# A fused long-convolution and SwiGLU kernel under another hand-written order of its operations

## The chip, the cores and the metric

The kernel runs on one core of a Trainium2 chip. The metric is the device time of one execution in microseconds (us); lower is better. The engines are TensorE (PE in the profile, its weight loads PEld), VectorE (DVE), ScalarE (ACT), GpSimd (POOL) and SyncE (SP); the last two issue the transfers here. Each engine works through its own instructions in order, and waits on semaphores for the others.

## The reference

All data are bf16; there are S = 2048 rows of D = 640 channels, and the hidden width of the second part is F = 1728.

```python
# A: shift convolution, long convolution, gate
k_shift = sum of 4 taps: k[t - i] * shift_k[:, i]
kv = k_shift * v
y  = irfft(rfft(kv, 2S) * rfft(ssm_k, 2S))[:S]   # causal convolution of 2048 taps, per channel
y  = y + kv * ssm_D
h  = q + layernorm(q) * y
# B: feed-forward
x2 = layernorm(h)
out = h + (silu(x2 @ w_gate) * (x2 @ w_up)) @ w_down
```

## The kernel before, in words

The sequence is cut into four blocks of 512 rows (`BLK`), block j = 0 to 3. Instead of one long FFT, each block of `ssm_k` and of `kv` has a spectrum of its own, made by matrix products with a cosine and sine matrix `WF`, and output block j sums the products of the spectra X_i and H_(j-i). In the names, G_j is the spectrum of block j of `ssm_k`, X_j that of block j of `kv`, and H_j is G_j joined with G_(j-1) (`window`, L463 and L467).

Per block the work is:

- `g_turned` brings a block of `ssm_k` with time on the partitions: for block 0 by TensorE transposes (L411) and evictions (L413), for the others by a ScalarE copy (L419, one instruction of 2560 columns) and transposing transfers.
- `kv_of` makes the shift convolution on TensorE (`taps`, L490) and multiplies by `v` on VectorE (L513 in block 0; else ScalarE eviction L511 and product L515).
- `transform` makes a spectrum: TensorE products (`forward`, L329) into a PSUM tile, and an eviction (`taken`, L319 on ScalarE, L322 if VectorE does it). Block 0 is done in two halves of 320 columns, `w0` and `w1`; the "first X eviction" is that of X0's tile c = 2 in half `w0`. Sums of halves are L361, L379, L386, L390 and L393 on VectorE.
- `mac` multiplies spectra on VectorE (L537 to L594; most products are 128x2560, L542 and L545).
- `inverse` goes back (TensorE L698), ScalarE scales by the first layer norm (L707), VectorE multiplies by q less its mean and so forms h (L709), ScalarE sums squares (L606), and VectorE and GpSimd make the second norm's statistics (L644, L646, L610, L648).
- `turn_h` normalises a row tile of h (L722 on ScalarE, or L724 if VectorE does it) and turns it into hT, by TensorE transposes with ScalarE evictions (L413) in blocks 0 and 3, by transposing transfers in blocks 1 and 2.
- `ffn` makes gate and up products (TensorE L769), SiLU (ScalarE L783), moves `up` out of PSUM (ScalarE L785) and multiplies on VectorE (L787); as an alternative VectorE multiplies straight from PSUM (L786) and L785 falls away. Then comes the down product (L833, L845), and the rows leave with an accumulating transfer (L850, L852), or at the end over L862, L864 and L866. The feed-forward part of block j lies among the convolution of block j+1.

Before all that stand some small preparations: `fold` (L886, L887) makes a small identity from the large one for the diagonal tap matrices (`tapw` L896, `diag` L897), and `negated` (L912) makes copies of `WF` and `WI` with the sign changed.

Nothing of this is emitted where it is written. `Plan.add` records 923 operations, and `Plan.run` emits them along the hand-written table `ORDER`; the order of the instructions on every engine is that of the table. A negative entry i is operation ~i run in its alternative form (another engine, or for L785 the product straight from PSUM). Buffers are given out along the same table, the one longest free first: four PSUM tiles of two banks (`ps`), five row tiles, three `sg` tiles and 22 units of a large SBUF array (`arena`). So the order of the table also sets which operation waits for which buffer.

## Time and profile before

| | |
|---|---|
| time, three runs | 252.25, 251.06 and 252.71 us; median 252.25 |
| profiled execution | 251.19 us, of which the span from first to last instruction is 249.5 us |
| TensorE busy | 237.7 us, 95% of the span |
| VectorE busy | 197.6 us, 79% |
| ScalarE busy | 174.0 us, 70% |
| GpSimd busy | 52.4 us, 21% |
| granted TensorE clock | 1.00 |
| read from and written to HBM | 16.29 MB and 4.59 MB |

A row of the timeline gives start, duration, engine, line, operation, tiles and shapes, and in brackets the idle time of the engine just before with what ended it. Neighbouring instructions of one line may share a row (x2 and so on). Matrix products overlap in the pipeline, so that the row of several ends a little after the next row begins. Idle time of an engine that nobody waits for costs nothing.

### The profile page before, as it was taken

How to read it: one execution, taken by the hardware profiler on the slowest of the kernel's cores; microseconds unless marked ns; L12 is line 12 of the kernel's file. 1: busy time of each engine (PE TensorE's matmuls, PEld its weight loads, DVE VectorE, ACT ScalarE, POOL GpSimd, SP SyncE). 2: the span in 40 equal slices, each digit the busy share in tenths (PEclk: the TensorE clock that was granted, in tenths of full speed). 3: DMA queues.
4: the chain of work that ended last, by engine and by line, in shares of the span. 5: the costliest groups of instructions: out<-in, count | busy, mean ns of one | idle time of the engine just before them, and what ended most of it. 6: DMA issues, size and time to landing. Idle time of an engine off the chain costs nothing.

```text
span 249.5 us, 5148 instructions
## 1 busy us (share of the span) xinstructions
PE 237.7 (95%) x2125; PEld 152.5 (61%) x2125; DVE 197.6 (79%) x250; ACT 174.0 (70%) x300; POOL 52.4 (21%) x53
## 2 busy tenths in 40 slices
PE   3899988999999999999999999999999999999994
PEld 3467655888857766544466676454456785464662
DVE  2779998999999999999999899999999542131222
ACT  2399998999999977969598699984532865325100
POOL 0002002531230313124400503353702110000030
PEclk9999999999999999999999999999999999999999
DMA  6999899287998566690725569789592200000052
GB/s 204 353 264 144 229 342 355 65 208 114 143 297 283 167 99 130 109 206 6 119 43 133 105 94 216 132 155 162 97 206 29 26 0 3 0 0 3 0 79 79
DMA packets 37283, 33.66 MB, mean 135 GB/s; under 512 B 22470, under 2 KB 32076, under 8 KB 37260
## 3 DMA queue, kind: packets, MB, share of 16 engines
q1 hardware_dynamic: 32028, 22.03, 34.0%
q0 software_dynamic: 5232, 11.31, 25.4%
q8 instruction: 16, 0.26, 0.4%
q14 instruction: 7, 0.06, 0.1%
HBM read 16.29 MB, written 4.59 MB: 84 GB/s over the span
## 4 chain that ended last, share of the span: by engine, by line
PE 75%; ACT 9%; DMA 6%; DVE 6%; issue 2%; SPq 1%; DVEq 0%; ACTq 0%
PE ps L769 36%; PE ps L845 23%; PE ps L329 7%; PE ps L698 5%; ACT arena L319 4%; DMA arena<-in_A_ssm_k_dram 4%; DMA arena<-arena 3%; PE ps L490 2%; DVE arena L542 2%; PE ps L833 1%; PE ps L411 1%; ACT arena L419 1%; DVE tT L787 1%; ACT sg L783 1%; ACT row L722 1%
## 5 line engine op out<-in xcount | busy, mean ns | idle before, releaser
L769 PE MATMUL ps<-arena,wgu 128*128 128x512 bf16 (+1 forms) x680 | 118.2, 329 | 0.4 <-ACT arena L413 0.2
L769 PEld LDWEIGHTS <-wgu 128*128 128x128 bf16 x680 | 66.2, 98 | 45.0 <-issue 1.1
L845 PE MATMUL ps<-wd,tT 128*128 128x320 bf16 x416 | 59.1, 299 | 0.0
L845 PEld LDWEIGHTS <-tT 128*128 128x128 bf16 x416 | 39.8, 98 | 17.2 <-issue 1.6
L542 DVE TENSOR_TENSOR arena<-arena 128x2560 bf16<-128x2560 bf16 x30 | 43.9, 1486 | 0.2
L783 ACT ACTIVATE sg<-ps 128x1024 bf16<-128x1024 f32 (+1 forms) x28 | 27.1, 971 | 22.2 <-PE ps L769 22.0
L329 PE MATMUL ps<-arena,WF 128*128 128x320 bf16 x176 | 29.8, 299 | 1.7 <-ACT arena L319 0.9
L785 ACT CAST sg<-ps 128x1024 bf16<-128x1024 f32 (+1 forms) x24 | 23.6, 982 | 8.5 <-PE ps L769 3.6
L610 POOL TENSOR_TENSOR sm<-sm,neghalf 128x4 f32<-128x4 f32 (+1 forms) x10 | 17.9, 1793 | 42.9 <-DVE sm L646 42.6
L243 POOL DMA_DIRECT2D arena<-arena x11 | 13.4, 1218 | 60.7 <-DVE arena L542 27.6
L319 ACT CAST arena<-ps 128x640 bf16<-128x640 f32 (+1 forms) x47 | 24.8, 594 | 1.3 <-PE ps L329 1.0
L787 DVE TENSOR_TENSOR tT<-sg,sg 128x1024 bf16<-128x1024 bf16 (+1 forms) x24 | 15.9, 664 | 11.0 <-ACT sg L785 11.0
L329 PEld LDWEIGHTS <-WF 128*128 128x128 bf16 x176 | 17.1, 97 | 11.1 <-issue 2.7
L545 DVE TENSOR_TENSOR arena<-arena 128x2560 bf16<-128x2560 bf16 x14 | 20.8, 1488 | 0.2
L606 ACT ACTIVATE junk<-arena 128x640 bf16<-128x640 bf16 x28 | 20.6, 745 | 0.4 <-DVE arena L709 0.4
L319 ACT ACTIVATE arena<-ps 128x640 bf16<-128x640 f32 (+1 forms) x32 | 19.8, 654 | 0.8 <-PE ps L329 0.8
L698 PE MATMUL ps<-arena,WI 128*128 128x320 bf16 x96 | 15.8, 299 | 1.0 <-issue 0.8
L709 DVE SCALAR_TENSOR_TENSOR arena<-arena,sm,ps 128x640 bf16<-128x640 bf16 x16 | 13.7, 877 | 3.2 <-ACT ps L707 3.1
L850 ACT ACTIVATE row<-ps,sm 128x640 bf16<-128x640 f32 x12 | 9.5, 791 | 8.6 <-PE ps L845 8.1
L852 POOL DMA_DIRECT2D out_dram<-row x12 | 11.7, 1151 | 14.6 <-ACT row L850 14.6
L707 ACT ACTIVATE ps<-ps,sm 128x640 f32<-128x640 f32 x16 | 11.9, 767 | 3.4 <-PE ps L698 3.3
L698 PEld LDWEIGHTS <-WI 128*128 128x128 bf16 x96 | 9.0, 97 | 5.6 <-issue 1.8
(91 smaller groups left out, 236.8 us busy)
## 6 DMA issues: line engine op xcount, KB each, us to landing
arena<-arena POOLq DMA_DIRECT2D x11, 640.0 KB, 6.2
arena<-in_A_v_dram SPq DMA_DIRECT2D x4, 640.0 KB, 5.1
arena<-in_A_q_dram SPq DMA_DIRECT2D x4, 640.0 KB, 4.5
out_dram<-row POOLq DMA_DIRECT2D x13, 160.0 KB, 4.2
arena<-in_A_ssm_k_dram SPq DMA_DIRECT2D x3, 640.0 KB, 8.8
wd<-in_B_w_down_dram SPq DMA_DIRECT2D x2, 800.0 KB, 7.1
out_dram<-arena POOLq DMA_DIRECT2D x2, 640.0 KB, 5.9
wgu<-in_B_w_gate_dram SPq DMA_DIRECT2D x1, 800.0 KB, 5.9
```

The lines of the kernel that those rows point to most:

```text
L319: (lambda: nc.scalar.activation(dst(), src(), ACT.Copy, scale=2.0)) if twice else (lambda: nc.scalar.copy(dst(), src())),
L329: nc.tensor.matmul(ap(ps)[:, h, 0:NH], w, ap(src)[:, r, h * NH:(h + 1) * NH], start=(first and i == 0), stop=(last and i == len(rs) - 1), ...
L542: dve(1402, lambda: v.tensor_mul(to(), X.part(xs), H.part(hs)), [X.at(xs), H.at(hs)], [at])
L545: added(1402 * n - 69 * (n - 1), lambda: v.tensor_add(to(), to(), b()), to, b, [what], at, n)
L606: act(725, lambda r=r: nc.scalar.activation(waste(), ap(x)[:, r, :], ACT.Square, scale=D ** -0.5, accum_out=sm(s, MSQ, (r,))), [(x, r)], [ ...
L610: nc.gpsimd.tensor_tensor(sm(s, RSTD, rs), sm(s, VAR, rs), ap(neghalf)[:, 0:len(rs)], op=ALU.pow)
L698: nc.tensor.matmul(ap(ps)[:, w, 0:NH], m, src[:, w * NH:(w + 1) * NH], start=(i == 0), stop=(i == len(terms) - 1))
L769: nc.tensor.matmul(split(ap(ps), n)[:, i, :], w(k), ap(hT)[:, k, lo:lo + n], start=(k == 0), stop=(k == KT - 1))
L783: act(905 if wide_ else 490, lambda: nc.scalar.activation(of(sg), of(*gate), ACT.Silu), [(gate[0], gate[1] + i) for i in range(m)] + (psu ...
L785: op = plan.add("act", 905 if wide_ else 490, lambda: nc.scalar.copy(of(co), of(*up)), psu + [sg], [co] + tt, ("dve", 1135 if wide_ else 6 ...
L787: op.rest = dve(602 if wide_ else 336, lambda: nc.vector.tensor_mul(to(), of(sg), of(co)), [sg, co], tt)
L845: nc.tensor.matmul(ap(ps[hf])[:, hf, 0:NH], ap(tT)[:, c * BLK + at:c * BLK + at + P], ap(wd)[:, c, hf * NH:(hf + 1) * NH], start=False, st ...
```

## The change

Only the table `ORDER` changes. It becomes one line shorter, so that every line below it has a number less by one in the changed kernel (L329 becomes L328, and so on). The operations are the same 923, and SyncE's and GpSimd's instructions, with all their transfers, keep their order. TensorE, ScalarE and VectorE work in another order in all blocks. Some operations go to the other engine or form:

- to VectorE: the first eviction of X0 (c = 2, half `w0`), the eviction of row tile 0 of block 0's turned `ssm_k`, and two normalisations of `turn_h` in block 2;
- to ScalarE: the eviction of row tile 3 of block 0's turned `ssm_k`, and one eviction of G0 (c = 2, half `w0`);
- product straight from PSUM: now for chunk 8 of block 1 and chunks 0 and 8 of block 3, no more for chunk 12 of block 2 and chunk 10 of block 3.

VectorE has 227 operations instead of 225, ScalarE 256 instead of 259.

```diff
 ORDER = (
-    0, 1, 2, 3, 16, 18, -20, 5, 4, 8, 17, 26, 13, 186, 9, 20, 22, 7, 10, 11, -22, 24, -26, 23, 75, 76, 77, 78, 79,
-    6, 193, 80, 81, 82, 30, 92, 93, 15, 12, 38, 83, 34, -40, 14, 36, 32, 35, 94, 27, -38, 95, 96, 97, 42, 28, 40,
...
+    0, 3, 16, 1, 4, 7, 2, 8, 9, 18, -20, 20, 10, 17, 22, 26, 5, 13, 186, 15, 12, 11, -22, 24, -26, 23, 75, 76, 77,
+    78, 6, 80, 193, 79, 81, 82, 92, -94, 94, 95, 38, -40, 14, 27, 34, -36, 42, 40, 41, 36, -38, 28, 30, 96, 97, 118,
...
```

What a row of the following lists holds is the line, the operation, the tile written and the tiles read, and the shape. First VectorE at the start of the program, from the first instruction that waits for block 0's k on (`kT` is k turned, `eye` the folded identity). Before:

```order
L413 COPY kT<-ps_72 128x5x128
L877 MEMSET kT 128x20
L886 TENSOR_TENSOR eye<-ident 128x64
L887 TENSOR_TENSOR eye<-eye 128x32
L896 COPY tapw<-ps_73 128x20
L897 TENSOR_TENSOR diag<-eye,tapw 128x640
L413 COPY kT<-ps_74 128x5x128
L413 COPY kT<-ps_72 128x5x128
```

And a little later, after the products with v (L513), before:

```order
L513 TENSOR_TENSOR arena<-ps_73,arena 128x2x4x32
L912 TENSOR_SCALAR arena<-WF 128x4x128
L413 COPY arena<-ps_72 128x640
L912 TENSOR_SCALAR arena<-WF 128x4x128
L413 COPY arena<-ps_73 128x640
```

The same stretch of VectorE with the change, without the four rows of products with v between its two parts:

```order
L885 TENSOR_TENSOR eye<-ident 128x64
L886 TENSOR_TENSOR eye<-eye 128x32
L412 COPY kT<-ps_73 128x5x128
L895 COPY tapw<-ps_72 128x20
L876 MEMSET kT 128x20
L896 TENSOR_TENSOR diag<-eye,tapw 128x640
```

```order
L512 TENSOR_TENSOR arena<-ps_72,arena 128x2x4x32
L321 TENSOR_SCALAR arena<-ps_73 128x320
L412 COPY arena<-ps_74 128x640
L412 COPY arena<-ps_75 128x640
L428 TENSOR_TENSOR arena<-arena 1x640
```

The fold now stands ahead of everything that waits for k, and the first X eviction (L321) stands on VectorE behind the last product with v, ahead of the evictions of the turned `ssm_k`; the negated copies of `WF` come later.

Second, VectorE where block 0's second half of columns comes out of the inverse and its first two row tiles are normalised (`row_64`, `row_65`; L709 and L724, now L708 and L723). Before:

```order
L515 TENSOR_TENSOR arena<-arena 128x2560
L709 SCALAR_TENSOR_TENSOR arena,sm_79<-arena,sm_76,ps_74 128x640
L709 SCALAR_TENSOR_TENSOR arena,sm_79<-arena,sm_76,ps_75 128x640
L648 SCALAR_TENSOR_TENSOR sm_78<-sm_78 128x2
L644 SCALAR_TENSOR_TENSOR sm_79<-sm_79 128x2
L724 TENSOR_SCALAR row_64<-arena,sm_78 128x640
L724 TENSOR_SCALAR row_65<-arena,sm_78 128x640
L467 TENSOR_TENSOR arena<-arena 128x2x1280
L463 TENSOR_TENSOR arena<-arena 128x2x1280
```

And with the change:

```order
L514 TENSOR_TENSOR arena<-arena 128x2560
L708 SCALAR_TENSOR_TENSOR arena,sm_79<-arena,sm_76,ps_73 128x640
L462 TENSOR_TENSOR arena<-arena 128x2x1280
L647 SCALAR_TENSOR_TENSOR sm_78<-sm_78 128x2
L708 SCALAR_TENSOR_TENSOR arena,sm_79<-arena,sm_76,ps_75 128x640
L723 TENSOR_SCALAR row_64<-arena,sm_78 128x640
L723 TENSOR_SCALAR row_65<-arena,sm_78 128x640
L466 TENSOR_TENSOR arena<-arena 128x2x1280
L643 SCALAR_TENSOR_TENSOR sm_79<-sm_79 128x2
```

The product of the window that stood behind the two normalisations (L463) now stands between the two products of the inverse (L462); the two row tiles of the inverse have changed places as well.

In the same place ScalarE: evictions of X1 (L319), the evictions of hT (L413 into `arena` from a transposed tile of 128x5x128) and the square sums (L606). Before:

```order
L319 CAST arena<-ps_72 128x640
L319 ACTIVATE arena<-ps_74 128x640
L413 COPY arena<-ps_75 128x5x128
L413 COPY arena<-ps_72 128x5x128
L319 CAST arena<-ps_74 128x640
L606 ACTIVATE junk,sm_79<-arena 128x640 x2
```

And with the change:

```order
L318 CAST arena<-ps_74 128x640
L318 ACTIVATE arena<-ps_73 128x640
L605 ACTIVATE junk,sm_79<-arena 128x640
L412 COPY arena<-ps_74 128x5x128
L412 COPY arena<-ps_75 128x5x128
L318 ACTIVATE arena<-ps_74 128x640
L605 ACTIVATE junk,sm_79<-arena 128x640
```

One of the two square sums has moved ahead of the two evictions of hT, for which the first feed-forward products wait.

Third, VectorE in block 2's inverse, among the feed-forward part of block 1. Before:

```order
L677 TENSOR_TENSOR arena<-arena 128x1280
L709 SCALAR_TENSOR_TENSOR arena,sm_82<-arena,sm_81,ps_73 128x640
L677 TENSOR_TENSOR arena<-arena 128x2x640
L709 SCALAR_TENSOR_TENSOR arena,sm_82<-arena,sm_81,ps_74 128x640
L787 TENSOR_TENSOR tT<-sg_70,sg_69 128x1024
L361 TENSOR_TENSOR arena<-arena 128x2560
L709 SCALAR_TENSOR_TENSOR arena,sm_82<-arena,sm_81,ps_74 128x640
```

And with the change:

```order
L676 TENSOR_TENSOR arena<-arena 128x1280
L708 SCALAR_TENSOR_TENSOR arena,sm_82<-arena,sm_81,ps_73 128x640
L786 TENSOR_TENSOR tT<-sg_70,sg_69 128x1024
L785 TENSOR_TENSOR tT<-sg_71,ps_74 128x1024
L708 SCALAR_TENSOR_TENSOR arena,sm_82<-arena,sm_81,ps_75 128x640
L360 TENSOR_TENSOR arena<-arena 128x2560
L708 SCALAR_TENSOR_TENSOR arena,sm_82<-arena,sm_81,ps_74 128x640
```

Two feed-forward products, one of them straight from PSUM (L785), now stand between the first and the second product of the inverse.

79 rows, old and new, of the table ORDER are left out of this document.

## The prediction

> **What bounds the kernel now.** I read the page's engine shares first, then the table of time stretches, then what TensorE waited for, then the timeline at the places where it waited.
>
> ```profile
> PE 237.7 (95%) x2125; PEld 152.5 (61%) x2125; DVE 197.6 (79%) x250; ACT 174.0 (70%) x300; POOL 52.4 (21%) x53
> PEclk9999999999999999999999999999999999999999
> PE 75%; ACT 9%; DMA 6%; DVE 6%; issue 2%; SPq 1%; DVEq 0%; ACTq 0%
> ```
>
> ```profile
> 12.81:30.00 17.19, 17.03 (x130) 11.77 (x130) 16.13 (x32) 16.75 (x43) 1.73 (x2) 1.00 0.97 201
> 30.00:39.20 9.20, 8.37 (x191) 5.90 (x190) 9.13 (x15) 8.21 (x20) 1.88 (x1) 1.00 1.03 343
> 39.20:43.83 4.63, 3.24 (x26) 1.87 (x24) 3.71 (x10) 4.43 (x8) 0.00 (x0) 1.00 1.08 354
> 43.83:78.08 34.25, 33.66 (x285) 27.16 (x285) 33.19 (x36) 33.48 (x56) 10.44 (x8) 1.00 0.75 169
> 78.08:120.00 41.92, 41.92 (x389) 24.92 (x389) 41.29 (x42) 35.42 (x63) 12.91 (x11) 1.00 0.62 136
> 120.00:160.00 40.00, 40.00 (x386) 24.33 (x384) 38.44 (x41) 33.54 (x60) 7.33 (x7) 1.00 0.67 124
> 160.00:190.40 30.40, 30.40 (x168) 15.49 (x166) 30.16 (x28) 16.39 (x22) 12.93 (x14) 1.00 0.72 132
> 190.40:246.00 55.60, 55.60 (x387) 35.96 (x385) 18.89 (x36) 21.69 (x32) 4.65 (x6) 1.00 0.12 22
> ```
>
> The columns of the second fence are the stretch, its length and the busy time of TensorE, its weight loads, VectorE, ScalarE and GpSimd. TensorE is idle for 249.5 - 237.7 = 11.8 us. From 78.08 to 246.00 it is never idle by its rows; the same number of matmuls is to be done there in any order, so an order can only lose there. What can be won lies ahead of 78.08, mostly ahead of 43.83, where the first feed-forward product starts. VectorE is the second engine: from 43.83 to 190.40 it is busy for 143.08 of 146.57 us. So where it gets more to do, TensorE may come to wait for it.
>
> ```profile
> PE ps L411 <- DMA arena<-in_A_k_dram: 4.0, 1, 4.0
> PE ps L411 <- DMA arena<-in_A_ssm_k_dram: 1.0, 1, 1.0
> PE ps L329 <- ACT arena L319: 0.9, 1, 0.9
> PE ps L698 <- issue: 0.8, 1, 0.8
> ```
>
> Of TensorE's idle time 4.0 us and then 1.0 us go to loads, which the change leaves as they are, and 0.8 us to no wait that the profile shows (the third matmul of an inverse, behind the same group in both orders). These 5.8 us I let stand, as well as the 3.5 us of the end behind the last matmul.
>
> **The change part by part.** Each part lays the measured durations end to end along the new order.
>
> *Start.*
>
> ```profile
> 5.17 0.17 DVE L886 TENSOR_TENSOR eye<-ident 128x64 bf16<-128x64 bf16 x1
> 5.38 0.18 DVE L887 TENSOR_TENSOR eye<-eye 128x32 bf16<-128x32 bf16 x1
> 10.91 2.51 ACT L419 COPY arena<-arena 128x2560 bf16<-128x2560 bf16 x1 [4.09 <-DMA arena<-in_A_ssm_k_dram]
> 11.35 0.43 PE L329 MATMUL ps<-arena,WF 128*128 128x320 bf16 x2 [0.18 <-DVE arena L513]
> 12.81 1.03 PE L411 MATMUL ps<-ident,arena 128*128 128x128 bf16 x15 [1.03 <-DMA arena<-in_A_ssm_k_dram]
> 13.31 0.46 ACT L319 ACTIVATE arena<-ps 128x320 bf16<-128x320 f32 x1
> 21.16 0.48 DVE L322 CAST arena<-ps 128x320 bf16<-128x320 f32 x1
> ```
>
> The two folds (0.17 and 0.18, with their overlap some 0.27) are done before k has landed, so the products with v end 0.27 earlier; but TensorE then waits for block 0's `ssm_k` until 12.81 anyway, and nothing of this stays. The first X eviction stood on ScalarE behind the copy of 2.51 us and ran at 13.31, though its products, begun at 11.35, were done at 11.78. On VectorE it takes about 0.48 (the eviction of that shape there; ScalarE took 0.46), is done at about 12.2, and the second pair of products of that tile fits into the wait that ended at 12.81: two matmul pairs less behind it, 0.27, with a stall of about 0.1 that goes. TensorE is 0.36 ahead at 14.2. VectorE gets 0.48 more here, but an eviction of that shape at 21.16 goes back to ScalarE and the copies of `WF` move behind. ScalarE has no less to do in sum, and from 14.2 to 37 it is nearly always busy (16.75 of 17.19 up to 30.00): of the 0.36 some 0.2 are left at 39. This hides in the next part; price alone nothing, from both sides -0.4 and +0.3 (one more eviction late on either engine).
>
> *Block 0 into its feed-forward part, 38 to 44 us.*
>
> ```profile
> 39.40 0.77 ACT L707 ACTIVATE ps<-ps,sm 128x640 f32<-128x640 f32 x1 [1.18 <-PE ps L698]
> 40.20 0.88 DVE L709 SCALAR_TENSOR_TENSOR arena<-arena,sm,ps 128x640 bf16<-128x640 bf16 x1 [0.93 <-ACT ps L707]
> 40.83 1.02 PE L329 MATMUL ps<-arena,WF 128*128 128x320 bf16 x6 [0.93 <-ACT arena L319]
> 41.20 0.80 DVE L724 TENSOR_SCALAR row<-arena,sm 128x640 bf16<-128x640 bf16 x2
> 42.48 1.30 ACT L413 COPY arena<-ps 128x640 bf16<-128x640 bf16 x2
> 43.31 1.49 DVE L463 TENSOR_TENSOR arena<-arena 128x2560 bf16<-128x2560 bf16 x1
> 43.83 0.97 PE L769 MATMUL ps<-arena,wgu 128*128 128x256 bf16 x7 [0.17 <-ACT arena L413]
> 44.22 0.78 ACT L606 ACTIVATE junk<-arena 128x640 bf16<-128x640 bf16 x1
> 44.95 0.77 ACT L606 ACTIVATE junk<-arena 128x640 bf16<-128x640 bf16 x1
> ```
>
> VectorE waited 0.93 us for ScalarE's scaling before its second product of the inverse (40.20). Now the window product of 1.49 us (L463 of before) stands in that gap. With the first product 0.2 earlier, it runs from about 39.0 to 40.5; the second product and the two normalisations follow, and these end at about 41.7 and 42.1, where they ended at 41.6 and 42.0. So nothing comes later by it, and VectorE is 0.9 ahead behind it. ScalarE, however, has a square sum ahead of the two evictions of hT. Two of these begin 44.95 - 44.22 = 0.73 us apart, and ScalarE has no gap there to hide it (4.43 busy of 4.63). The evictions of 42.48 so begin at about 43.1 to 43.2, and the first feed-forward product at 44.55 instead of 43.83: **+0.72 us**. If the cover is another than I think (the transposes late instead), it is +0.3; at the other end, with TensorE 0.2 ahead and the wait of 0.93 before 40.83 shortened by it, +0.5; if the rows of hT also come late by the window product's 1.49 less the 0.93, +1.3.
>
> *Feed-forward of block 0's first chunks beside block 1's convolution, 43.83 to 78.08.*
>
> ```profile
> 56.19 1.01 ACT L785 CAST sg<-ps 128x1024 bf16<-128x1024 f32 x1 [0.21 <-DVE tT L787]
> 67.73 1.49 DVE L582 TENSOR_TENSOR arena<-arena 128x2560 bf16<-128x2560 bf16 x1 [0.41 <-DMA arena<-arena]
> 70.98 0.70 PE L329 MATMUL ps<-arena,WF 128*128 128x320 bf16 x4 [0.31 <-ACT sg L785]
> 76.53 1.45 PE L698 MATMUL ps<-arena,WI 128*128 128x320 bf16 x8
> 78.08 0.82 PE L769 MATMUL ps<-arena,wgu 128*128 128x256 bf16 x6
> ```
>
> By the rows TensorE is idle for 34.25 - 33.66 = 0.59 us here; by the distance of the starts the stalls are more, since a row hides about 0.16 of each (matmuls of 320 columns follow each other after 0.13 to 0.14 us, as the two of 11.35 show, which take 0.43 where one takes 0.30; eight that nothing holds up take about 1.09 to the next group, and those of 76.53 took 78.08 - 76.53 = 1.55). Added up over all groups in this way they come to 1.65 us. In the new order VectorE has its 0.93 us lead and I find four stalls left, 0.61 us in all, the largest 0.41 at the matmuls that now stand in place of those of 70.98, behind an `up` eviction on ScalarE. So **-1.04 us**, and with the 0.05 by which the group behind them closes up, TensorE at 78.08 is 0.72 - 1.09 = -0.37 us, that is 0.37 ahead. The bounds: all 1.65 gone on one side; on the other none, because ScalarE is busy for 33.48 of the 34.25 us and has no room to catch up.
>
> *Behind 78.08.* Two stalls of about 0.12 and 0.11 us (at 89.1 and 104.2 by the starts, too short to show as idle time) are not there when I lay out the new order: -0.23. Apart from that TensorE's work is the same and the stretch is full, provided that VectorE keeps up. VectorE gets more: two normalisations of block 2 (0.80 for two of that kind at 41.20), and in block 2's inverse the product straight from PSUM.
>
> ```profile
> 213.70 1.22 DVE L786 TENSOR_TENSOR tT<-sg,ps 128x1024 bf16<-128x1024 bf16 x1 [3.86 <-PE ps L769]
> L787 DVE TENSOR_TENSOR tT<-sg,sg 128x1024 bf16<-128x1024 bf16 x22 | 15.1, 686 | 11.0 <-ACT sg L785 11.0
> ```
>
> That costs 1.22 instead of 0.69 us, so +0.53; in sum 1.33 us up to about 160, against a lead of 0.93 and the 0.41 of waiting at 67.73 that goes. The two cancel, and I let TensorE lose nothing. The products straight from PSUM in block 3 lie behind 190.40, where VectorE is busy for 18.89 of 55.60 us. Transfers follow their producers: GpSimd's and SyncE's order stands, and where VectorE or ScalarE is earlier by up to 0.9 us, so are they.
>
> *Sum.* +0.72 - 1.09 - 0.23 = -0.60 us. I take -0.5, since a layout by hand leaves out the small waits. The profiled execution took 251.19 us (span 249.5, 1.69 around it), so 250.7 after; it stood 1.06 below the median of the runs shown, and by that median the forecast is **251.7 us**. The runs shown lie 1.65 apart; a measurement tells a change from none at about 1%, 2.5 us.
>
> **The clock.** In all stretches the granted clock is 1.00, and TensorE's longest idle time after its start is 1.03 us (12.81). The Trainium skill, "TensorE: Matmul & The Clock Gate", section "HAM oscillation", says that an idle gap of more than about 3.4 us puts TensorE back to half its clock. By that rule this change would cost nothing unless it opens such a gap; the trace has none, so no run here shows it.
>
> **The rivals.** *VectorE runs out of lead (slower).* If the 0.93 us at 40.20 is not won, VectorE comes 1.33 us later to the two places where TensorE waits for its results in blocks 2 and 3: the inverse of block 2, where the product straight from PSUM now stands ahead of three of four products of the inverse (the PSUM tiles of these are held meanwhile, and the down products need them), and X3, which waits for the product with v. It decides from the point at which VectorE's lead there falls under about 0.4 us, my estimate of the slack from the laid-out rows. Then TensorE loses up to 1.33, and the +0.72 with nothing won back comes on top: 251.19 + 0.72 + 1.33 = 253.2, or 254.3 by the median; up to 256 if both places also hold up ScalarE. For it speaks VectorE's 41.29 of 41.92 us; against it that it is idle 1.56 us from 120 to 160.
>
> *The late start stays (near no change).* ScalarE has no room from 43.83 to 78.08, so +0.72 remains: 253.0.
>
> *The early stalls go (faster).* With 0.16 hidden in each, the idle 1.39 us between 39.20 and 43.83 (four stalls) are 2.0, and the 0.16 between 12.81 and 30.00 (two, near its end) about 0.5; with 1.65 and 0.23 that is 4.4. If the new order takes them all, 251.19 - 4.4 = 246.8, or 247.8 by the median. Against it speak the load, ScalarE's fullness and the square sum ahead of the evictions.
>
> *A gap that lowers the clock.* A new stall over three times as long as the longest shown (1.03), 3.5 us, and work at a lower clock behind it: at least 3.5, so 255.8 by the median. With that page's figures, half the clock for another 3.4 us, the estimate is 1.7 more, 257.5.
>
> *It does nothing that can be seen* (no lead, no late start): 252.25, inside the forecast's own range.
>
> **How the numbers follow.** The forecast with its own range 250.4 to 252.5, "nothing" included: 0.51. The late start stays (252.5 to 253.7): 0.15. VectorE runs out of lead (253.7 to 256): 0.19. The early stalls go (247.5 to 250.4): 0.13. The clock: 0.02. One per cent of 252.25 is 249.7 to 254.8. Faster takes most of the early stalls, 0.12; slower takes over half of VectorE's case and the clock, 0.13; the rest, 0.75, is the same. The range 249.6 to 255.1 leaves out about 0.11 below and 0.09 above.
>
> **What would show it.** Right: a first feed-forward product (L768) at about 44.5; the window product (L462) without a wait before it near 39; the X0 eviction on VectorE (L321) near 11.8 and its second products ahead of the wait for `ssm_k`; TensorE at the start of the next chunk (78.08 before) some 0.4 earlier; no idle time of TensorE behind it. Wrong: TensorE idle in block 2's inverse (about 132 to 140) or ahead of X3 (about 157) with VectorE as releaser; or a longer wait ahead of 44, if the transposes of hT come late; or stalls of 1 us and more in block 1's inverse.

## The result and the profile after

Over 20 runs each the changed kernel took 254.01 us (median; 251.81 to 257.99) and the kernel before 252.13 (250.39 to 254.79). The ratio is 1.0078, with a 95% interval from 1.0053 to 1.0102: slower by 0.8%, about 2.0 us, where 0.5 us faster was forecast. The ratio is taken without the slowest runs of either kernel. The time lies inside the range, on the wrong side of no change. All rows of the changed kernel below are from its second profiled execution (254.31 us, span 252.6), unless another kernel is named. From the page, the engine shares, the granted clock and the chain:

```profile
PE 238.2 (94%) x2113; PEld 152.8 (61%) x2125; DVE 198.7 (79%) x252; ACT 172.2 (68%) x297; POOL 58.3 (23%) x53
PEclk9999999999999999999999999999999999999999
PE 68%; ACT 11%; DMA 10%; DVE 7%; issue 3%; SPq 0%; ACTq 0%; POOLq 0%; DVEq 0%
```

TensorE's share of the chain fell from 75% to 68%, and that of transfers rose from 6% to 10%, though no transfer was touched. GpSimd is busy for 58.3 instead of 52.4 us. Its instructions are the same.

The stretches, cut where TensorE starts the same work as in the table before (the columns are the same too; a dozen of TensorE's matmul records are missing in this trace, so its busy time reads up to 0.4 us low):

```profile
15.87:32.12 16.25, 15.50 (x108) 10.14 (x108) 15.21 (x30) 15.47 (x41) 3.02 (x2) 1.00 0.88 154
32.12:40.77 8.65, 8.27 (x189) 5.97 (x189) 8.44 (x14) 8.50 (x20) 1.53 (x1) 1.00 0.80 251
40.77:46.04 5.27, 3.21 (x25) 1.87 (x25) 5.27 (x11) 5.12 (x10) 0.51 (x1) 1.00 1.07 350
46.04:80.55 34.51, 32.98 (x284) 27.10 (x284) 32.28 (x35) 32.70 (x53) 14.52 (x8) 1.00 0.80 195
80.55:248.58 168.03, 166.96 (x1312) 100.50 (x1321) 129.52 (x146) 104.96 (x172) 38.16 (x36) 1.00 0.51 93
```

Three of these rows answer terms of the sum. 40.77 to 46.04, from the first product of X1 to the first feed-forward product, is 5.27 us long, where before it was 43.83 - 39.19 = 4.64: +0.63 (forecast +0.72). 46.04 to 80.55 is 34.51, against 34.25: +0.26 (forecast -1.04). Behind 80.55 there are 168.03 us; before, from 78.08 to the same last matmul at 245.43, 167.35: +0.68 (forecast -0.23). A fourth loss was not in the forecast at all, in the first row. What TensorE waited for shows it:

```profile
PE ps L328 <- DMA arena<-arena: 2.0, 2, 1.4
PE ps L328 <- ACT arena L318: 1.6, 2, 1.1
PE ps L328 <- DVE arena L321: 0.9, 1, 0.9
PE ps L768 <- ACT sg L782: 0.4, 1, 0.4
```

The first line is new. It is two waits of TensorE for transposing transfers out of the `arena`, 0.58 us at 25.01 and 1.44 us at 64.94.

For comparing kernels I use four points at which TensorE has done the same operations in both orders: behind 15 (an X0 product), 48 (in the middle of G1), 54 (block 1's taps) and 134 (the end of block 1's inverse; 78.08 before) of its 329. Times between their starts in us, from each kernel's timeline; the last column ends at the last matmul:

| kernel | 15 to 48 | 48 to 54 | 54 to 134 | 134 to end |
|---|---|---|---|---|
| before | 11.30 | 3.90 | 48.01 | 167.36 |
| before, executed again | 11.30 | 3.90 | 46.91 | 167.44 |
| changed, first profile | 12.79 | 3.75 | 48.12 | 169.36 |
| changed, second profile | 12.49 | 3.75 | 48.44 | 168.03 |

By the last row against the first, the changed kernel loses 1.19 - 0.15 + 0.43 + 0.67 = 2.1 us behind the 15th operation. One execution doesn't settle such a figure: the first profile of the changed kernel (an execution of 255.87 us) loses 3.45 us in the same way, and the kernel before executed again took 1.1 us less in the third column. Ahead of the 15th operation the time belongs to the execution, not to the order: the nine 512-wide matmuls at the very start (L882) took from 2.05 to 3.49 us, and the 15th operation began between 14.6 and 18.2 us over all kernels here, in either order (the 18.2 with a granted clock of 0.50 just ahead of it, told further down).

### The profile page after: what moved, and what is told of

Read it like the earlier page. It is cut to its first block, busy times and chain, and to the rows that moved or that the text cites. A ratio compares the mean times of both kernels' runs of the same rounds, so it can differ in the third digit from the quotient of the medians.

```text
span 254.2 us, 5165 instructions
## 1 busy us (share of the span) xinstructions
PE 239.8 (94%) x2125; PEld 152.7 (60%) x2125; DVE 198.6 (78%) x252; ACT 172.4 (68%) x297; POOL 58.6 (23%) x53
## 4 chain that ended last, share of the span: by engine, by line
PE 36%; DVE 34%; DMA 16%; ACT 8%; issue 3%; SPq 2%; ACTq 0%; DVEq 0%; POOLq 0%
PE ps L844 14%; PE ps L768 13%; DMA arena<-arena 10%; DVE arena L541 9%; DVE arena L544 5%; DVE tT L786 3%; ACT arena L318 3%; DMA arena<-in_A_v_dram 3%; DMA wgu<-in_B_w_up_dram 2%; PE ps L697 2%; PE ps L328 2%; DVE arena L661 2%; DVE arena L662 2%; DMA arena<-in_A_k_dram 2%; PE ps L410 2%
## 5 line engine op out<-in xcount | busy, mean ns | idle before, releaser
L782 ACT ACTIVATE sg<-ps 128x1024 bf16<-128x1024 f32 (+1 forms) x28 | 27.0, 967 | 17.3 <-PE ps L768 14.5
L328 PE MATMUL ps<-arena,WF 128*128 128x320 bf16 x176 | 29.9, 299 | 5.2 <-ACT arena L318 1.6
L784 ACT CAST sg<-ps 128x1024 bf16<-128x1024 f32 (+1 forms) x23 | 22.1, 960 | 14.0 <-DVE tT L786 7.7
L609 POOL TENSOR_TENSOR sm<-sm,neghalf 128x4 f32<-128x4 f32 (+1 forms) x10 | 20.5, 2052 | 45.3 <-DVE sm L645 45.0
L318 ACT CAST arena<-ps 128x320 bf16<-128x320 f32 (+1 forms) x48 | 25.2, 579 | 2.7 <-PE ps L328 2.6
L328 PEld LDWEIGHTS <-WF 128*128 128x128 bf16 x176 | 16.9, 97 | 15.7 <-issue 5.2
L786 DVE TENSOR_TENSOR tT<-sg,sg 128x1024 bf16<-128x1024 bf16 (+1 forms) x23 | 14.9, 649 | 7.2 <-ACT sg L784 7.2
L318 ACT ACTIVATE arena<-ps 128x640 bf16<-128x640 f32 (+1 forms) x31 | 19.1, 662 | 0.8 <-PE ps L328 0.8
L851 POOL DMA_DIRECT2D out_dram<-row x12 | 12.8, 1261 | 10.8 <-ACT row L849 10.8
L708 DVE SCALAR_TENSOR_TENSOR arena<-arena,sm,ps 128x640 bf16<-128x640 bf16 x16 | 13.7, 874 | 0.9 <-ACT ps L706 0.9
L785 DVE TENSOR_TENSOR tT<-sg,ps 128x1024 bf16<-128x1024 bf16 (+1 forms) x5 | 5.6, 1113 | 10.6 <-ACT sg L782 5.5
```

The lines of the kernel that those rows point to most:

```text
L318: (lambda: nc.scalar.activation(dst(), src(), ACT.Copy, scale=2.0)) if twice else (lambda: nc.scalar.copy(dst(), src())),
L328: nc.tensor.matmul(ap(ps)[:, h, 0:NH], w, ap(src)[:, r, h * NH:(h + 1) * NH], start=(first and i == 0), stop=(last and i == len(rs) - 1), ...
L609: nc.gpsimd.tensor_tensor(sm(s, RSTD, rs), sm(s, VAR, rs), ap(neghalf)[:, 0:len(rs)], op=ALU.pow)
L782: act(905 if wide_ else 490, lambda: nc.scalar.activation(of(sg), of(*gate), ACT.Silu), [(gate[0], gate[1] + i) for i in range(m)] + (psu ...
L784: op = plan.add("act", 905 if wide_ else 490, lambda: nc.scalar.copy(of(co), of(*up)), psu + [sg], [co] + tt, ("dve", 1135 if wide_ else 6 ...
L786: op.rest = dve(602 if wide_ else 336, lambda: nc.vector.tensor_mul(to(), of(sg), of(co)), [sg, co], tt)
```

## The experiments

In the diffs an entry of `ORDER` is an operation's number. Beside these runs the kernel before had medians of 251.57 to 251.90 us. Kernels with a pin have four more lines, so that L403 is L407 there.

**Both kernels again, and the buffer.** SyncE's order is the same, but look at when it issues the first transposing transfer of block 1's `ssm_k`. The first fence is the kernel before, the second the changed kernel, the third the changed kernel with one pin (columns as ever; SPq is SyncE's queue).

```profile
13.45 1.29 SPq L404 DMA_TRANSPOSE arena<-arena  x1
28.77 0.33 SPq L296 DMA_DIRECT2D arena<-in_A_v_dram  x1
```

```profile
11.38 2.49 ACT L418 COPY arena<-arena 128x2560 bf16<-128x2560 bf16 x1 [4.34 <-DMA WF<-const_wf]
15.64 1.30 SPq L403 DMA_TRANSPOSE arena<-arena  x1
25.01 0.45 PE L328 MATMUL ps<-arena,WF 128*128 128x320 bf16 x2 [0.58 <-DMA arena<-arena]
33.18 0.33 SPq L295 DMA_DIRECT2D arena<-in_A_v_dram  x1
```

```profile
13.69 1.29 SPq L407 DMA_TRANSPOSE arena<-arena  x1
24.40 1.36 PE L332 MATMUL ps<-arena,WF 128*128 128x320 bf16 x8
```

Its source, ScalarE's copy, is there at 11.38 + 2.49 = 13.87; the transfer leaves 1.8 us later. Units of the `arena` are given out along `ORDER`, and the new order makes the turned block of `ssm_k` (operation 194) take unit 4, which the TensorE transposes of block 0's `ssm_k` still read. All that SyncE issues behind it is late as well. The pin gives it unit 10, which nobody reads any more; the second experiment then also makes the later load of `v` wait as it does in the change.

```diff
+PIN = {194: 10}            # second experiment: {194: 10, 191: 4}
-                    b.at = arena.take(b.size) if b.pool == "U" else idle[b.pool].pop(0)
+                    b.at = arena.take(b.size, PIN.get(op.n) if b.size == 1 else None) if b.pool == "U" else ...
```

The changed kernel again:

> The changed kernel as it is. Buffer theory (the changed order hands out other SBUF units, so that the first transposing transfer of block 1's turned ssm_k waits for a TensorE transpose and the load of block 1's v waits for the last product of block 0, and the whole SyncE queue runs 2 to 5 us later): in every profile the first L403 transfer is issued 1.5 to 2.5 us after the end of the L418 copy, and the load of v some 4 us or more later than 28.8. Rival, a clock that starts late (nine warm-up matmuls of L881 took 3.55 us in the profile of the changed kernel and 2.12 in that of before): then those nine take about 3.5 us again. If they take about 2.1 here, their 1.4 us belong to the execution and not to the order. Time 1.004 to 1.012 of before.

On unit 10:

> The changed order, but the unit of the turned ssm_k of block 1 is another one, long free (unit 10 instead of 4); by that the load of block 1's v falls into the unit of that tile, as in the kernel before. Buffer theory: the first L403 transfer is issued right behind the copy (about 13.5 to 14.0), the load of v about 2 to 3 us earlier than in the changed kernel, the stall of about 1 us ahead of G1's second forward matmuls (25.6) goes, and the time falls by 0.7 to 1.5 us, to 1.002 to 1.005 of before. Rival, VectorE running out of lead behind 78 us: the stalls at 105 to 200 us stay and the time falls by less than 0.4 us.

On unit 10, with `v` late:

> As the run with another unit for the turned ssm_k, but the load of block 1's v is put behind the last product of block 0's spectra (VectorE L593), as in the changed kernel. This tells the two buffer waits apart. If only the wait of the turned ssm_k costs time, this run is as fast as the other (within 0.3 us); if the late load of v and the weights behind it cost, it is 0.5 us or more slower than the other.

The kernel before again:

> The kernel before once more, for its profile. If the warm-up clock belongs to the execution, the nine matmuls of L882 take 2 to 3.6 us here, with no fixed value; the stalls of TensorE between 80 and 246 us stay under 0.4 us in sum.

Measured: 1.0112 [1.0065, 1.0160] for the changed kernel again, 1.0070 [1.0037, 1.0103] on unit 10, 1.0073 [1.0039, 1.0107] with `v` late, and one run of 250.49 us of the kernel before. On unit 10 the stall ahead of G1's first product is gone and the 15th to the 48th operation takes 11.74 us instead of 12.49 (11.73 with `v` late): by these profiles 0.75 us of the front's loss is that buffer, and 0.44 us stay with the order; against the first profile (12.79) the buffer is 1.05. The late `v` costs nothing. The medians don't settle it: the intervals overlap, 1.0070 lies above the 1.002 to 1.005 that were expected, and the first comparison gave the changed kernel itself 1.0078.

**Parts of the order.** Two hybrids keep the order of before up to a point and go on with that of the change, a third does the reverse, and a fourth moves only the first X eviction to VectorE.

```diff
# start_before_rest_after: the change's order from TensorE's 48th operation on
-129, 188, 202, 203, 131, 134, 214, 215, ...
+129, 188, 202, 203, 134, 131, 209, 210, ...
# to_78_before_rest_after: from the 134th on
-280, 183, 284, 285, 365, 369, 295, 368, ...
+280, 183, 284, 285, 379, 500, 412, 365, ...
# start_after_rest_before: the change up to the 48th, before from there (lines of the change)
-197, 127, 208, 212, 202, 203, 130, 134, ...
+197, 127, 208, 212, 130, 128, 213, 190, ...
# before_93_on_DVE
-81, 82, 30, 92, 93, 15, 12, 38, ...
+81, 82, 30, 92, -94, 15, 12, 38, ...
```

> The order of before up to the forward matmul of G1 that starts at 26.17 us there, and the changed order behind it. Theory of the start (the changed start costs 0.7 us by the X0 eviction and 0.5 to 1.2 by the buffer wait of block 1's turned ssm_k): the time falls from 1.011 to 1.004 to 1.006 of before. Rival, all of the loss lies behind 78 us: it stays at 1.008 or more.

> The order of before up to the feed-forward matmuls that start at 78.08 us there, and the changed order behind. It shows what the back part alone costs. By the profiles 0.5 to 0.9 us: 1.002 to 1.004. By the prediction's rival (VectorE out of lead) 1.3 to 2 us: 1.005 to 1.008.

> The changed order up to the same forward matmul of G1 (26.17 us in before), and the order of before behind it. Theory of the start: 1.2 to 1.9 us slower than before, 1.005 to 1.007. If the start is free, as the prediction had it, 0.999 to 1.001.

> The order of before, with the first X eviction alone moved to VectorE, at its place behind the first copy of WF. It gives what the named step does by itself. Theory: its second products stay behind the transposes on TensorE, so nothing waits for it and the time is 0.998 to 1.002. Rival: VectorE is late by it and the turned ssm_k with it, 0.3 to 0.5 us slower, 1.001 to 1.002. If the step is a gain, 0.4 us faster, 0.998.

| kernel | ratio, interval | 15 to 48 | 48 to 54 | 54 to 134 | 134 to end |
|---|---|---|---|---|---|
| start_before_rest_after | 1.0058 [1.0020, 1.0096] | 11.38 | 3.98 | 48.07 | 168.05 |
| to_78_before_rest_after | 1.0048 [1.0014, 1.0083] | 11.30 | 3.90 | 48.55 | 168.18 |
| start_after_rest_before | 1.0008 [0.9979, 1.0037] | 12.84 | 3.77 | 47.06 | 167.34 |
| before_93_on_DVE | 1.0023 [0.9993, 1.0054] | 11.30 | 3.90 | 48.12 | 167.34 |

The last column goes with the order behind 78 us alone: 167.34 to 167.44 in that of before, 168.03 and more in that of the change. That stretch by itself makes the kernel slower. The front loses its time in the trace (12.84), but not in the median, where 1.005 to 1.007 were expected; from the 15th operation to the end its profile has 231.01 us, those of the kernel before 230.57 and 229.55. The eviction on VectorE alters no stretch.

**Single places put back.** On the changed kernel with unit 10, one place each, and then all together:

```diff
# mid_window_back: window product (219) and square sum (156) behind what they had passed
-235, 219, 178, 236, ...           154, 156, -162, 162, 163, -165, 165, 166, 240, ...
+235, 178, 236, ...                154, -162, 162, 163, -165, 219, 165, 166, 156, 240, ...
# mid_turn_h_early: two ScalarE sums of block 1 (269, 266) behind block 0's normalisation 167
-244, 269, 266, 255, ...           323, 167, 171, ...
+244, 255, ...                     323, 167, 269, 266, 171, ...
# back_product_early: product 485 ahead of 593
-463, 464, 593, -482, 468, 480, 482, 408, 469, 563, 566, 485, ...
+463, 464, 485, 593, -482, 468, 480, 482, 408, 469, 563, 566, ...
```

> The changed order with the other unit for block 1's turned ssm_k, and in block 0's second half the window product (L462 of 1.49 us on VectorE) again behind the two normalisations, and the square sum (L605) again behind the two evictions of hT. Theory: in the changed kernel the window product delays the rows of hT by about 1.1 us and the square sum the evictions by 0.7, so the first feed-forward product comes 4.4 to 4.6 us after the first forward matmul of X1 instead of 5.2, and TensorE is 0.7 to 1.2 us earlier there; by the chain behind it at most part of this reaches the end: 0.3 to 1.0 us, time 1.003 to 1.006. Rival: the delay is taken up by the waits behind, and the time stays at 1.007.

> The changed order with the other unit, and two sums of block 1's first norm (L628, L630, 1.8 us on ScalarE) behind the two normalisations of turn_h in block 0 instead of ahead. Theory: those normalisations are the last readers of the unit into which block 2's turned ssm_k is transposed, so its transfers start 0.8 to 1.2 us earlier and the stall of 0.8 to 1.7 us ahead of G2's forward matmuls (63 to 65 us) falls by as much. Rival: the stall comes from TensorE's own order or from the transfers' length, and stays.

> The changed order with the other unit, and in block 2 one product of spectra (L541 on VectorE) two products earlier, as in before. Theory: GpSimd's accumulating transfer of that product is issued about 3 us earlier, VectorE's wait of 0.4 us for it near 116 us goes, the copy of block 3's ssm_k on ScalarE (L418, which waits 2.1 us for VectorE) starts 0.4 to 1 us earlier, and TensorE's stall of 0.39 us at 121 to 123 goes; the stretch from 78 us (first L768 group of chunks 8 to 11) to the group at 121 shrinks from 42.3 to 41.8 to 42.0 us. Rival: VectorE is too late there anyway and the stall stays.

> The changed order with the other unit and with the three moves of the runs beside it. If these four places carry the loss, the time is 0.999 to 1.003 of before; if the loss is spread over places not touched, 1.004 to 1.007.

Measured: 1.0066 [1.0038, 1.0094], 1.0097 [1.0060, 1.0134], 1.0120 [1.0067, 1.0173] and 1.0080 [1.0051, 1.0108]. None brings the time back, and all four together don't come near the 0.999 to 1.003 that were expected if these places carry the loss. The window product and the sums put back change where TensorE stalls: the stall ahead of G2's first product is gone, but with the sums moved there is one of 0.72 us at 59.80. From the 54th to the 134th operation the first two and the last took 47.80, 49.87 and 48.22 us. The 49.87 can't be compared with the others, because the granted clock fell in that execution (a digit is a slice of 6.3 us; from 42.9 to 46.3 us it was 0.50):

```profile
PEclk9999998899999999999999999999999999999999
```

Product 485 is the instructive one, taken up with the next group.

**The order's parts with the first loss mended.**

```diff
# mid_only_from_change: before, with the change's order from the 48th to the 134th operation
-129, 188, 202, 203, 131, 134, 214, 215, ...
+129, 188, 202, 203, 134, 131, 209, 210, ...
# start15_only_from_change: the change up to the 15th, then before (lines of the change)
-30, 96, 97, 118, 88, 89, 84, 85, ...
+30, 96, 97, 118, 83, 32, 88, 89, ...
# start48_good_unit: start_after_rest_before with
+PIN = {194: 10}
# before_product_485_late: before, with one product moved
-484, -482, 485, 460, 480, 592, 408, 591, 590, 593, 463, 564, 461, 468, 582, 482, 464, ...
+484, -482, 460, 480, 592, 408, 591, 590, 593, 463, 564, 461, 468, 582, 482, 485, 464, ...
```

> The kernel before, with the change's order of TensorE, ScalarE and VectorE only between TensorE's 48th operation and the end of block 1's inverse (26 to 78 us). If the change loses in this stretch by its own order (theory: window product between the two products of block 0's inverse, G2's products ahead of transfers that come late): this stretch is 0.5 to 0.9 us longer than before's 47 to 48 us, ratio 1.002 to 1.004, while the stretch behind 78 stays at 167.35 us. If the loss of the stretch comes only from what the front hands on (transfers 2 to 5 us later): ratio 1.000 and 47 to 48 us.

> The change's order only up to TensorE's 15th operation (X0's first eviction on VectorE included), the order of before from there; the turned block of ssm_k gets another unit than the awaited one. Theory (the start is worth nothing, the loss lies behind it): TensorE's 15th to 48th operation takes 11.30 us, behind 78 us 167.35, and the ratio is 0.997 to 1.001. Rival (the start itself loses by VectorE's later copies of WF): the stretch behind the 15th operation is over 11.5 us, ratio above 1.002.

> The change's order up to TensorE's 48th operation with the turned block of ssm_k on a unit that nobody reads (10), the order of before behind it. The same hybrid on unit 4 took 12.84 us from the 15th to the 48th operation. Theory of the buffer wait: 11.74 us here, no stall of about 1 us ahead of G1's first product at 25, ratio 0.996 to 0.999. If that wait is only a symptom and the order itself costs the time: 12.6 us and more, ratio 1.001.

> The kernel before with one VectorE instruction moved: the second sum of block 1's spectra products (the product whose result goes into the accumulating transfer) stands behind the next three, as in the change. If this place alone costs the 0.36 us that the change loses between 85 and 120 us: that stretch is 35.3 to 35.4 us instead of 35.03. If it takes the other unit and the later VectorE as well (the copy of block 3's ssm_k has another unit here): 35.03 to 35.1 us. The rest stays.

| kernel | ratio, interval | 15 to 48 | 48 to 54 | 54 to 134 | 134 to end |
|---|---|---|---|---|---|
| mid_only_from_change | 1.0027 [0.9996, 1.0057] | 11.30 | 3.98 | 47.61 | 167.28 |
| start15_only_from_change | 1.0008 [0.9976, 1.0040] | 11.46 | 3.90 | 48.04 | 167.37 |
| start48_good_unit | 1.0002 [0.9975, 1.0029] | 11.74 | 3.77 | 47.51 | 167.35 |
| before_product_485_late | one run, 254.21 us | 11.30 | 3.89 | 47.40 | 169.27 |

The unit again makes 12.84 into 11.74, and no median tells the difference (1.0008 and 1.0002). In mid_only_from_change the 54th to the 134th operation took 47.61 us, within the 47 to 48 that were expected if the middle loses nothing by its own order; what this owes to GpSimd is the subject of the last group. None of these hybrids beats the kernel before. The last row is the clear one: one VectorE instruction, moved behind the next three of its queue as in the change, costs 1.9 us behind 78 us in its one execution. The change loses 0.7 us there in its second profile and 2.0 in its first. The expectation had 0.36 us at most. The rows of before, of the changed kernel and of this one at that place:

```profile
103.50 1.20 POOL L243 DMA_DIRECT2D arena<-arena  x1 [4.25 <-PE ps L329]
115.09 2.58 ACT L419 COPY arena<-arena 128x2560 bf16<-128x2560 bf16 x1
```

```profile
109.38 1.20 POOL L242 DMA_DIRECT2D arena<-arena  x1 [8.89 <-DVE arena L541]
116.18 1.49 DVE L541 TENSOR_TENSOR arena<-arena 128x2560 bf16<-128x2560 bf16 x1 [0.42 <-DMA arena<-arena]
119.11 2.59 ACT L418 COPY arena<-arena 128x2560 bf16<-128x2560 bf16 x1 [2.10 <-DVE arena L544]
122.67 2.53 PE L768 MATMUL ps<-arena,wgu 128*128 128x512 bf16 x11 [0.45 <-ACT sg L782]
```

```profile
108.22 1.20 POOL L242 DMA_DIRECT2D arena<-arena  x1 [7.84 <-PE ps L768]
115.10 1.49 DVE L541 TENSOR_TENSOR arena<-arena 128x2560 bf16<-128x2560 bf16 x1 [2.00 <-DMA arena<-arena]
118.15 2.58 ACT L418 COPY arena<-arena 128x2560 bf16<-128x2560 bf16 x1 [1.81 <-DVE arena L544]
121.71 0.59 PE L768 MATMUL ps<-arena,wgu 128*128 128x512 bf16 x2 [0.57 <-ACT sg L782]
129.86 0.70 PE L328 MATMUL ps<-arena,WF 128*128 128x320 bf16 x4 [0.38 <-ACT sg L784]
```

Read it as a chain. The result of product 485 goes into GpSimd's accumulating transfer. Counted from the start of the stretch (78.08, 80.55 and 79.21 us in the three kernels) this leaves 3.4 and 3.6 us later than in before. In the changed kernel its source is the only unit free when VectorE's next large product takes one, so VectorE stands (116.18; 115.10 in the third). The copy of block 3's `ssm_k` takes a unit that VectorE frees behind that, so ScalarE stands for 2 us; SiLU queues behind it, and TensorE waits for SiLU. In before the copy ran at 115.09 without a wait. Putting 485 back in the changed kernel takes this stall away and opens another one:

```profile
127.03 1.49 DVE L665 TENSOR_TENSOR arena<-arena 128x2560 bf16<-128x2560 bf16 x1 [0.67 <-DMA arena<-arena]
130.97 0.72 PE L701 MATMUL ps<-arena,WI 128*128 128x320 bf16 x4 [0.42 <-DVE arena L677]
```

That is block 2's inverse, whose scratch unit a transposing transfer still reads. The stretch behind 78 us took 168.20 us. Against the 168.69 of the kernel on unit 10 without this move half a us is gained, against the 168.03 of the changed kernel nothing.

**GpSimd in the middle.** From the first feed-forward product to the end of block 1's inverse the kernels with the change's order there have two lengths. The windows of mid_only_from_change, of back_product_early when executed again, of the one on unit 10, and of the changed kernel (in its row above, 34.51):

```profile
45.24:78.41 33.17, 32.93 (x286) 27.33 (x285) 32.23 (x35) 32.32 (x53) 9.38 (x8) 1.00 0.72 170
```

```profile
45.46:78.64 33.18, 32.89 (x285) 27.35 (x285) 32.10 (x35) 32.33 (x53) 9.39 (x8) 1.00 0.71 168
```

```profile
45.16:79.01 33.85, 33.01 (x285) 27.12 (x284) 32.00 (x35) 32.67 (x53) 14.89 (x8) 1.00 0.68 165
```

The fifth busy time, GpSimd's, tells them apart: 9.4 us and 14.5 to 14.9. It is one instruction, the power in block 0's second statistics, a mere 128x2. The changed kernel, and statistics_waited_early, whose diff stands below:

```profile
48.93 6.15 POOL L609 TENSOR_TENSOR sm<-sm,neghalf 128x2 f32<-128x2 f32 x1 [7.66 <-DVE sm L645]
53.05 1.48 DVE L389 TENSOR_TENSOR arena<-arena 128x2560 bf16<-128x2560 bf16 x1
55.12 0.16 DVE L647 SCALAR_TENSOR_TENSOR sm<-sm 128x2 f32<-128x2 f32 x1 [0.59 <-POOL sm L609]
59.89 4.49 SPq L403 DMA_TRANSPOSE arena<-arena  x3
64.94 0.45 PE L328 MATMUL ps<-arena,WF 128*128 128x320 bf16 x2 [1.44 <-DMA arena<-arena]
```

```profile
47.34 0.88 POOL L613 TENSOR_TENSOR sm<-sm,neghalf 128x2 f32<-128x2 f32 x1 [7.66 <-DVE sm L649]
48.25 0.16 DVE L651 SCALAR_TENSOR_TENSOR sm<-sm 128x2 f32<-128x2 f32 x1 [0.59 <-POOL sm L613]
51.96 7.40 SPq L407 DMA_TRANSPOSE arena<-arena  x3
```

```diff
# statistics_waited_early: unit 10, and VectorE's L647 (160) four instructions earlier
-331, 249, 239, 334, ...           327, 160, 170, ...
+331, 249, 160, 239, 334, ...      327, 170, ...
```

> The change's order with the turned block of ssm_k on unit 10, and one VectorE instruction of 128x2 (L647 of the change, the one that waits for GpSimd's power of block 0's second statistics) moved up behind the first of the five sums and products that stood before it; no buffer changes. In the same kernel without this move GpSimd's power of 128x2 took 6.15 us, from 47.76 to just after the end of VectorE's products at 53.36. Theory (GpSimd's instruction is kept from its data as long as VectorE's two-operand products follow each other, and the transfers behind it keep block 2's turned ssm_k waiting): with VectorE standing still early the power takes 0.7 to 1.5 us, the transposing transfers of block 2's ssm_k start before 54 instead of at 57.9, no stall of 0.76 us ahead of G2's first product, and from the first feed-forward product to the end of block 1's inverse it takes 33.1 to 33.3 us instead of 33.84. Rival (the length of the power instruction is only how it is recorded, or its code is fetched late): it stays at 6 us and the transfers stay late. Ratio 1.003 to 1.006 by the theory, 1.007 by the rival.

> The same kernel as in the run with the product moved early (the change's order, unit 10, operation 485 ahead of 593), executed anew. There the power of 128x2 took 0.88 us, although up to there its order is that of the kernel in which it took 6.15. If what it takes is settled from execution to execution by a race between GpSimd and VectorE: 6.15 is possible here, with a stall ahead of G2's first product and 33.8 to 34.5 us from the first feed-forward product to the end of block 1's inverse; if it belongs to the kernel: 0.88 us and 33.15 us again. Ratio 1.005 to 1.010 in either case.

Measured: the power took 0.88 us in both, the stretch 33.14 and 33.18 us, the ratios are 1.0072 [1.0047, 1.0096] and 1.0105 [1.0073, 1.0136]. In the first, then, power and stretch came out as the theory had them, but the ratio as the rival had it. Where the power takes 6.15 us it ends as VectorE's row of products ends (53.05 + 1.48 = 54.53, power's end 55.08); the outgoing transfer queued behind it frees its unit late, block 2's transposing transfers leave at 58 to 60 instead of 52 us, and G2's first product stalls for 0.6 to 1.6 us. Over the nine executions with the change's own order in this stretch (statistics_waited_early, with its one move, among them), the five with 6.15 us took 33.85 to 35.23 us and the four with 0.88 us 33.14 to 33.18. That the long power causes the late transfers, and these the stall, the rows show. A short power is not all that it takes: mid_window_back and all_four_back, in another order here, had 0.88 us and took 33.85 and 34.24. What makes the power long is not settled. The early wait went with 0.88, but so did mid_only_from_change and both executions of back_product_early without it. The two kernels that were executed twice with the change's order in this stretch gave the same length twice (6.16 and 6.15; 0.88 and 0.88), so it seems to go with the kernel rather than with the execution; yet up to this place the order and the units of back_product_early are those of the kernel on unit 10, which took 6.15. The Trainium skill, "SBUF — State Buffer", section "SBUF: two separate sides", says that GpSimd and a VectorE instruction with two inputs from SBUF exclude each other, and that the later one waits for the other's end. The 6.15 us agree with it in kind; it doesn't tell why five VectorE instructions go ahead of GpSimd in one kernel and not in another.

## Why the prediction was wrong

- **"TensorE 0.36 ahead at 14.2"**, priced at nothing: the price held, as far as it can be seen. The eviction stands on VectorE, but behind a product with v that came late in this execution, and TensorE waits for it; the 15th operation's time varies by more than the term.

```profile
12.98 0.76 DVE L512 TENSOR_TENSOR arena<-ps,arena 128x256 bf16<-128x256 f32 x2 [1.37 <-PE ps L489]
13.65 0.48 DVE L321 TENSOR_SCALAR arena<-ps 128x320 bf16<-128x320 f32 x1
14.18 0.43 PE L328 MATMUL ps<-arena,WF 128*128 128x320 bf16 x2 [0.95 <-DVE arena L321]
```

- **"Transfers follow their producers: GpSimd's and SyncE's order stands"**: this step failed first. The order stands, the buffers do not. The front of the document says that units are given out along the table; the prediction named no wait that follows from it. One new unit cost 0.75 to 1.1 us between 15 and 28 us by the profiles (12.49, 12.79 and 12.84 with it, 11.74 without), and the order there 0.44 more.
- **Block 0 into its feed-forward part, +0.72**: right in size. From the first X1 product to the first feed-forward product it takes 5.27 to 5.55 us in the change's order, 4.37 to 4.64 in that of before. The reason was only half right:

```profile
39.23 1.49 DVE L514 TENSOR_TENSOR arena<-arena 128x2560 bf16<-128x2560 bf16 x1
40.63 0.88 DVE L708 SCALAR_TENSOR_TENSOR arena<-arena,sm,ps 128x640 bf16<-128x640 bf16 x1
41.43 1.49 DVE L462 TENSOR_TENSOR arena<-arena 128x2560 bf16<-128x2560 bf16 x1
42.91 0.88 DVE L708 SCALAR_TENSOR_TENSOR arena<-arena,sm,ps 128x640 bf16<-128x640 bf16 x1
43.83 0.74 ACT L605 ACTIVATE junk<-arena 128x640 bf16<-128x640 bf16 x1
46.04 1.14 PE L768 MATMUL ps<-arena,wgu 128*128 128x256 bf16 x9
```

  The square sum does stand ahead of the evictions of hT. But the window product (41.43) fills no gap: VectorE works without a break, so the second product of the inverse, ready to go at 41.43, starts 1.48 us later. In the second execution of before the gap of 0.93 us wasn't there either, nor was the wait of 0.8 us put down to "issue"; a lead that rests on one wait of one execution was none.
- **43.83 to 78.08, -1.04**: right where nothing else intervened, 33.14 to 33.18 us against 34.25, that is -1.07 to -1.11. In the changed kernel (34.20 and 34.51 in its two profiles) the long power of GpSimd took 1.0 to 1.4 us of it away, through transfers again.
- **Behind 78.08, -0.23, "provided that VectorE keeps up"**: it didn't, +0.68 in the second profile and +2.0 in the first; the twelve profiles with the change's order there have 168.03 to 169.36 us. The rival that VectorE runs out of lead named the right engine and too high a price (1.33), at the wrong places: TensorE stalled at 122.67, on an `up`-and-SiLU queue that a displaced product had held up over a transfer, a unit and a copy. The two moved normalisations and the product straight from PSUM, on which the price was worked out, do not stand in that chain. In the first profile TensorE also stalled ahead of X3, a place that the rival had named; but VectorE, which it waited for, had itself waited 1.84 us for the load of `v`:

```profile
160.71 1.49 DVE L514 TENSOR_TENSOR arena<-arena 128x2560 bf16<-128x2560 bf16 x1 [1.84 <-DMA arena<-in_A_v_dram]
162.25 0.43 PE L328 MATMUL ps<-arena,WF 128*128 128x320 bf16 x2 [0.25 <-DVE arena L514]
```

- **The clock**: in both profiles of the changed kernel the granted clock is 1.00 in every stretch, and no new gap comes near 3.5 us. The loss is there without the clock: the changed kernel's 16 timed runs with a mean granted clock of 0.995 or more have a median of 254.07 us, the 111 such runs of the kernel before 251.64. But the sign that the prediction named, such a gap, is not needed. In mid_turn_h_early the granted clock was 0.50 for 3.4 us behind waits of TensorE of 0.93 and 1.11 us, and in start_before_rest_after for 3.4 us from 14.9 us on, in a wait of 1.82 us:

```profile
PEclk9979999999999999999999999999999999999999
```

  One such stretch makes a mean of 0.993. A mean under 0.995 came in 10 of 121 timed runs of the kernel before, in 8 of 62 of the kernels with its order between the 48th and the 134th operation, and in 40 of 116 of those with the change's order there, places put back or not. In before these runs are longer (254.19 against 251.64), in the first 20 of the changed kernel they are not (8 with 253.7, 12 with 254.1). So the new order goes with a lower clock more often; the prediction gave this 0.02, by a gap that did not come. Why it is so, no run here shows.

With the second profile of the changed kernel and the first of the kernel before, the parts add up: 1.19 between the 15th and the 48th operation (0.75 the unit, 0.44 the order), 0.15 back at the taps, 0.47 back from there to the first X1 product (9.12 us before, with the 0.8 us of "issue" in it, 8.65 now), 0.63 up to the feed-forward part, 0.26 in it (1.08 won, 1.34 lost to GpSimd) and 0.68 behind 78 us: 2.1 us, against 2.0 in the medians, in which a start of 14.6 to 18.2 us floats. That the two agree is in part luck, since the changed kernel's first profile gives 3.45. Of these the loss behind 78 us is shown by medians of its own (1.0048); those of the front and the middle are shown by the traces of each kernel, while the medians of their hybrids can't be told from 1. The kernel with 485 put back is no better in the medians (1.0105 and 1.0120) than the changed one, though its profiled executions are 2 us shorter. A part of this is the clock: five of its ten runs had a mean under 0.995, with a median of 254.86 us, and the other five have 252.81, against 254.07 in such runs of the changed kernel. With all four places put back 1.0080 is left, so most of the loss in the medians is not traced to single places.

## What to carry to other kernels

Where buffers are handed out along the order of the work, a new order is also a new allocation: before pricing it, list for each operation whose buffer it inherits and who still reads that one, above all for instructions that issue transfers, since all that stands behind them in their queue is late too. Follow every moved producer through its transfer to the next owner of its buffer; here one product moved by three places cost 1.9 us in the kernel before, four links further down. And don't build a term on a single idle time of a single execution: read it in two, each with its granted clock beside it.

## What the runs showed of the hardware

A GpSimd instruction of 128x2 took 0.88, 3.42 or 6.15 us at the same place of the program, in steps that go with VectorE's row of products: 3.42 in all eight profiled executions with the order of before there, and 6.15 or 0.88 with the change's. The nine 512-wide matmuls of the start took 2.05 to 3.49 us up to the next group, though the row of the granted clock shows nines there. Behind 78 us, in contrast, all seven profiled executions with the order of before lie between 167.28 and 167.44 us, so that a single profile resolves there what 12 timed runs of the whole kernel cannot; the twelve with the change's order spread over 1.3 us. The granted clock fell to 0.50 for 3.4 us with no wait of TensorE over 1.11 us in the 30 us ahead of it in one execution (mid_turn_h_early), and stayed at 1.00 behind a wait of 2.50 us in another (before_product_485_late, ahead of 14.81).
